# Split attention scores: three single-pass products of high and low parts in place of one four-pass float32 product, and a new table for the order of the work

## The chip, the cores and the metric

The kernel runs on one core of one Trainium2 chip. The metric is the device time of one launch in microseconds (us). Before the change the median of three runs is 1307.7 us (1306.86 to 1309.71).

## The reference

Eight batches of eight heads of attention over 576 tokens with head size 64, in which only scores within `tau` of a row's largest score take part, and then a gated layer over the 4608 tokens (512 wide, 1536 inside):

```python
scores = scale * np.matmul(q, k.transpose(0, 1, 3, 2))
thresh = np.max(scores, axis=-1, keepdims=True) - tau
scores = np.where(scores >= thresh, scores, -1000000000.0)
scores = scores - np.max(scores, axis=-1, keepdims=True)
attn = np.exp(scores)
attn = attn / (np.sum(attn, axis=-1, keepdims=True) + 1e-09)
out = np.matmul(attn, v)            # then (batch, token, head*64) as x
gate = 1.0 / (1.0 + np.exp(-(x @ w_gate)))
val = x @ w_val
return (gate * val @ w_out)
```

## The kernel before

**Attention.** There are 32 visits, one for each batch and each pair of heads; visit n is batch n // 4, pair n % 4. A visit has nine score tiles of 128 query rows by 576 keys: four for each head, and one in which the 64 leftover rows of both heads stand together. q and k come from memory with the head's 64 numbers on 64 partitions, and the two halves of the 576 keys lie on partitions 0 to 63 and 64 to 127. So a tile is computed by two matmuls of 64x128 by 64x288, one on each half of TensorE's rows (line 641); the leftover tile takes four. They are float32 matmuls, and the trace has two records for each. A visit thus has ten pairs of such matmuls and 40 records. After a tile, VectorE takes the row's largest score (L648) and the threshold (L657), ScalarE the exponential (L662), VectorE masks and sums (L665), TensorE turns the result (L756, evicted by ScalarE in L704) and multiplies it by v (L795). GpSimd multiplies a finished visit by the reciprocals of the row sums (L695), which make a round trip through memory to be spread over partitions (tiles `rd` and `rb`).

`plain_scores` loads k (two tiles `kp`, one for each head) and q (`qp`, both heads) and multiplies q by 1/8 in place: on ScalarE or, for visits 1, 2, 4 and all from 6 on, on GpSimd (L621, two instructions a visit).

**The gated layer.** Its products are taken as three fp32r products: an operand is written as a high part (a copy to the type fp32r) and a low part (the operand minus the high part, a subtraction on GpSimd or VectorE), and high x high, high x low and low x high are summed. Part of it stands between the visits: block 0 (L937 in, L866 out), blocks 1 and 2 (L892 in; L866 out, tiles `gpp` and `wpair`), the first two kinds in row halves as well. Blocks 3 to 8 come behind attention in three pairs (L1213 and L1355). The weights come in a packed form and are first converted (`convert`, 36 times, two VectorE instructions each, L528 and L534), and sums of weights and of activations that the pairs need are made on GpSimd (L1071, L1083, L1121, L1126).

**The order.** Every operation is recorded with an engine, a cost and a key. `Plan.run` plays them through with these costs and gives each engine's instructions a fixed order: of the ready operations the one with the smallest key for which there is room in the buffers (`SLOTS`, a number of buffers for each tag). The DMAs all stand in one queue, SP's. Keys of attention are the number of the tile since the start; the gated layer's matmuls have keys from a million up, so they fill what attention leaves. `held_by` ties a visit's scores to the progress of the gated layer. `LAG` is how long a result is taken to need to another engine, `SWITCH` what a change between TensorE's row, column and full forms is taken to cost. Each visit has a seed (`ORDERS`), and all keys below 398 of that visit are moved by random numbers up to 3 drawn from it (`vary`).

The names that the rows below use: `kp`, `qp` are k and q of a visit, `p` the probabilities, `pt` their transposes, `xf` a visit's output, `x` and `wi` the operands of blocks 0 to 2, `s` and `s_o` the sums of weights, `st` the row maxima and thresholds.

Of the kernel before, what the change touches and what calls it, by code (L numbers as in the profile page):

```python
# [4 lines left out]

# [39 lines left out]
class Plan:  # L45

    IN_TURN = ("x", "xf", "kd", "qd", "vs", "p", "pt", "pl", "ptc")

    def __init__(self, pools, slots):
        self.pools, self.slots = pools, slots
# [4 lines left out]
    def buf(self, tag, shape, dtype, name, cls=None):  # L57
        return Buf(self, tag, shape, dtype, name, cls)
# [40 lines left out]
        self.ops.append(o)  # L99
        return o  # L100

    def vary(self, seed):

        draw = random.Random(seed)
        self.nudge = (lambda: draw.uniform(-NUDGE, NUDGE)) if seed else lambda: 0.0

    def room(self, o):
        need = {}
# [150 lines left out]
EARLY = 16  # L259
AHEAD = 5  # L260

PAD = 64

def Q_BY(pair):
    return "POOL" if pair in (1, 2, 4) or pair > 5 else "ACT"
# [25 lines left out]
def LO_DVE(j, out):  # L291
# [2 lines left out]

DVE_LO_IN, DVE_LO_OUT = (), ()

LAG = {"PE": 0.3, "DVE": 0.06, "ACT": 0.08, "POOL": 0.12, "SP": 0.08}

WARM = 16

# [3 lines left out]
    "s": [{0, 1}, {2, 3}, {4, 5}, {6, 7}],  # L304
    "b": [{6}, {7}, {4}, {5}, {2}, {3}, {0}, {1}],
}
STAY, SWITCH, TURN = 4, 0.15, 0.0615
S_CAP, T_CAP, L_CAP, MOE_CAP = (4, 3), 1, 1, 2

MM_HALVES = 0.234  # L310
WHOLE, FULL_STEP = (0,), 6

ORDERED, NUDGE = 398, 3.0
ORDERS = (
    9752, 0, 748, 1675, 6489, 1465, 5011, 3559, 9165, 5460, 4071, 9213, 3320, 7371, 6555, 4493,
    0, 1253, 2636, 4108, 9865, 7590, 738, 2276, 1215, 1549, 3530, 2072, 647, 565, 5179, 0,
)

def LATE(b, hp):
# [21 lines left out]
def act(n):  # L341
    return 0.19 + 0.0008 * n
# [6 lines left out]
def pool(n):  # L349
    return 0.2 + 0.0022 * n  # L350
# [7 lines left out]
def kernel(  # L358
# [208 lines left out]
    class Visit:  # L567
# [28 lines left out]
        def plain_scores(self, key, n):  # L596

            pair = 4 * self.b + self.hp
            self.k1 = [buf("qd", [P, HALF + SL], F32, f"kp{n}_{h}") for h in range(2)]
            qn = self.q1 = buf("kd", [P, 2, SK], F32, f"qp{n}")  # L600

            pieces = [(0, 2 * P), (2 * P, SK)] if n == "0_0" else [(0, SK)]
            for hs in [(0,), (1,)] if n == "0_0" else [(0, 1)]:
                for x in hs:
                    op("SP", 0.7, key - 4 + x, lambda x=x: nc.sync.dma_start(out=self.k1[x].ap, in_=k0[pair, :, x]),
                       writes=[self.k1[x]])
                h = slice(hs[0], hs[-1] + 1)
                for j, (c0, c1) in enumerate(pieces if 0 in hs else [(0, SK)]):
                    parts = [(qn, (x, y)) for x in hs for y in ((j,) if len(pieces) > 1 and 0 in hs else (0, 1))]
                    op("SP", 1.05 * len(hs) * (c1 - c0) / SK, key - 4, lambda h=h, c0=c0, c1=c1: nc.sync.dma_start(  # L610
                        out=qn.ap[:, h, c0:c1], in_=q0[pair, :, h, c0:c1]
                    ), writes=parts)
            for h in range(2):
                for j, (c0, c1) in enumerate(pieces if h == 0 else [(0, SK)]):
                    dst = [(qn, (h, y)) for y in ((j,) if len(pieces) > 1 and h == 0 else (0, 1))]
                    if Q_BY(pair) == "ACT":
                        op("ACT", act(c1 - c0), key + h, lambda h=h, c0=c0, c1=c1: nc.scalar.activation(
                            qn.ap[:, h, c0:c1], qn.ap[:, h, c0:c1], AF.Copy, scale=scale_t[:, 0:1]
                        ), writes=dst)
                        continue  # L620
                    op("POOL", 0.89, key + h, lambda h=h, c0=c0, c1=c1: nc.gpsimd.tensor_scalar(  # L621
                        out=qn.ap[:, h, c0:c1], in0=qn.ap[:, h, c0:c1], scalar1=scale_t[:, 0:1], scalar2=zero_t[:, 0:1],
                        op0=ALU.mult, op1=ALU.add,
                    ), writes=dst)

    def tile_steps(vis, g, i, key):

        h, qt = g.h, g.tiles[i]
        n = f"{g.name}{i}"


# [13 lines left out]

        op("PE", P_COST * len(heads), key, scores, reads=reads, writes=[s], also=[g.p], after=held_by(vis), mode="row")
# [747 lines left out]
    def two_blocks(k):  # L1394

        key = 400 + k
        tags = ["x"] * 6 + ["vs"] * 2 + ["kd"] * 3 + ["p"] * 3
        if k in xs_d:
            tags = ["kd"] * 3 + ["p"] * 3 + ["vs"] * 2 + ["x"] * 6
# [8 lines left out]
                b, d = xt[prod][c].b, xs_d[k][prod, c]  # L1408
                op("SP", 1.7, key, lambda b=b, d=d: nc.sync.dma_start(out=f32(b.ap), in_=d.t), reads=[d], writes=[b])
        else:  # L1410
            base = {}
            tags = iter(["qd"] * 6 + ["xf"] * 2)
            for hp in (0, 2, 1, 3):
                for z in range(2):
                    base[hp, z] = pair_x(k, hp, z, next(tags), key)
# [189 lines left out]
```

## Time and profile before

| | before |
|---|---|
| median of 3 runs | 1307.7 us |
| profiled execution | 1305.66 us |
| its span, first to last instruction | 1303.6 us |
| TensorE (PE) busy | 1265.9 us, 97% |
| VectorE (DVE) busy | 892.8 us, 68% |
| ScalarE (ACT) busy | 685.4 us, 53% |
| GpSimd (POOL) busy | 512.8 us, 39% |
| granted TensorE clock, mean | 0.993 |

The profiled execution took 2.06 us more than its span, and is 2.04 us below the median. "PEld" is TensorE's weight loads, which have a record each and run beside the matmuls. Matmuls overlap one another in TensorE's pipeline, so the mean length of a matmul's record is not the time that it takes from the engine; that is read from the distance between the starts of groups in the chain of waits.

### The profile page before, as it was taken

How to read it: one execution, taken by the hardware profiler on the slowest of the kernel's cores; microseconds unless marked ns; L12 is line 12 of the kernel's file. 1: busy time of each engine (PE TensorE's matmuls, PEld its weight loads, DVE VectorE, ACT ScalarE, POOL GpSimd, SP SyncE). 2: the span in 40 equal slices, each digit the busy share in tenths (PEclk: the TensorE clock that was granted, in tenths of full speed). 3: DMA queues.
4: the chain of work that ended last, by engine and by line, in shares of the span. 5: the costliest groups of instructions: out<-in, count | busy, mean ns of one | idle time of the engine just before them, and what ended most of it. 6: DMA issues, size and time to landing. Idle time of an engine off the chain costs nothing.

```text
span 1303.6 us, 27638 instructions
## 1 busy us (share of the span) xinstructions
PE 1265.9 (97%) x10596; PEld 997.8 (77%) x10596; DVE 892.8 (68%) x1811; ACT 685.4 (53%) x1144; POOL 512.8 (39%) x501
## 2 busy tenths in 40 slices
PE   7879999999999999999999999999999999999998
PEld 5557777777777777777777767888888888888887
DVE  7878887576776766767777774548954579555494
ACT  6877776666665656665776651224522235312242
POOL 4567777665444366584868400111001100010100
PEclk8989999999999999999999999999999999999999
DMA  7669986677655767887446668666676666765663
GB/s 284 218 216 305 337 283 218 225 263 237 234 191 180 236 222 255 288 296 227 156 146 202 222 222 295 195 201 209 221 270 195 198 206 203 232 197 188 203 208 113
DMA packets 134571, 293.17 MB, mean 225 GB/s; under 512 B 27304, under 2 KB 62376, under 8 KB 134440
## 3 DMA queue, kind: packets, MB, share of 16 engines
q1 hardware_dynamic: 134296, 291.41, 67.5%
q8 instruction: 84, 1.38, 0.4%
q14 instruction: 47, 0.39, 0.1%
q10 hardware_dynamic: 144, 0.00, 0.0%
HBM read 229.34 MB, written 62.01 MB: 224 GB/s over the span
## 4 chain that ended last, share of the span: by engine, by line
PE 86%; DMA 3%; DVE 3%; POOL 2%; ACT 2%; issue 2%; SPq 1%; DVEq 0%; POOLq 0%; ACTq 0%
PE banks L1213 26%; PE banks L1355 13%; PE banks L795 11%; PE banks L892 11%; PE banks L641 10%; PE banks L756 5%; PE banks L866 5%; PE banks L937 4%; DMA rb<-rd 1%; DVE p L665 1%; ACT pt L704 1%; DMA xa<-xf 1%; DVE st L648 1%; DMA sod<-s_o 0%; DMA qp<-in_q_dram 0%
## 5 line engine op out<-in xcount | busy, mean ns | idle before, releaser
L648 DVE TENSOR_REDUCE st<-banks 128x1 f32<-128x576 f32 x256 | 190.3, 753 | 142.3 <-PE banks L641 136.5
L665 DVE SCALAR_TENSOR_TENSOR p<-banks,st,p 128x576 f32<-128x576 f32 x256 | 205.0, 813 | 25.2 <-ACT p L662 18.3
L641 PE MATMUL banks<-kp,qp 64*128 64x288 f32 x1280 | 204.2, 424 | 12.9 <-DVE p L665 6.5
L662 ACT ACTIVATE p<-banks,st 128x576 f32<-128x576 f32 x256 | 186.7, 742 | 49.8 <-DVE st L648 48.4
L1126 POOL TENSOR_TENSOR gA<-gA 128x512 f32<-128x512 f32 x18 | 24.2, 1347 | 412.9 <-DVE gA L1192 412.9
L892 PE MATMUL banks<-x,wi 64*128 64x512 f32 x1152 | 178.6, 423 | 3.5 <-DVE g L998 2.5
L1355 PE MATMUL banks<-gs_p,wo_p 128*128 128x512 f32 x756 | 172.3, 389 | 0.0
L1355 PEld LDWEIGHTS banks<-gs_p,wo_p 128*128 128x128 f32 x756 | 141.9, 188 | 29.4
L641 PEld LDWEIGHTS banks<-kp,qp 64*128 64x128 f32 x1280 | 113.5, 189 | 49.7 <-DVE p L665 14.5
L704 ACT COPY pt<-banks 128x1024 f32<-128x1024 f32 x128 | 129.5, 1012 | 35.3 <-PE banks L756 33.3
L892 PEld LDWEIGHTS banks<-x,wi 64*128 64x128 f32 x1152 | 111.3, 186 | 25.9 <-DVE g L998 5.1
L795 PE MATMUL banks<-pt,vs 128*64 128x256 f32 x1024 | 124.7, 386 | 5.6 <-DVE p L665 3.9
L756 PEld LDWEIGHTS banks<-ident,p 64*128 64x128 f32 x2304 | 98.2, 141 | 35.3 <-DVE p L665 5.1
L1150 DVE TENSOR_TENSOR qu<-banks,qp 128x512 f32<-128x512 f32 x72 | 49.8, 692 | 92.9 <-PE banks L1213 74.4
L756 PE MATMUL banks<-ident,p 64*128 64x64 f32 x2304 | 106.1, 227 | 6.1 <-DVE p L665 2.6
L1213 PE MATMUL banks<-xs_p,wa 128*128 128x512 f32 x432 | 110.2, 390 | 0.0
L1213 PE MATMUL banks<-xs_p,wt 128*128 128x512 f32 x432 | 109.2, 389 | 0.0
L795 PEld LDWEIGHTS banks<-pt,vs 128*64 128x64 f32 x1024 | 69.9, 138 | 47.2 <-DVE p L665 5.9
L1213 PE MATMUL banks<-xs_p,ws 128*128 128x512 f32 x432 | 104.1, 390 | 0.0
L1213 PEld LDWEIGHTS banks<-xs_p,wa 128*128 128x128 f32 x432 | 80.8, 188 | 17.8 <-issue 1.2
L1213 PEld LDWEIGHTS banks<-xs_p,ws 128*128 128x128 f32 x432 | 80.9, 188 | 17.5 <-issue 0.7
L1213 PEld LDWEIGHTS banks<-xs_p,wt 128*128 128x128 f32 x432 | 81.1, 188 | 16.9
(125 smaller groups left out, 1991.0 us busy)
## 6 DMA issues: line engine op xcount, KB each, us to landing
wi<-wid SPq DMA_DIRECT2D x48, 512.0 KB
qp<-in_q_dram SPq DMA_DIRECT2D x31, 640.0 KB
wa<-wid SPq DMA_DIRECT2D x36, 512.0 KB
ws<-sid SPq DMA_DIRECT2D x36, 512.0 KB
wt<-sid SPq DMA_DIRECT2D x36, 512.0 KB
wo_p<-sod SPq DMA_DIRECT2D x36, 512.0 KB
wo_p<-wod SPq DMA_DIRECT2D x27, 512.0 KB
vs<-in_v_dram SPq DMA_DIRECT2D x32, 384.0 KB
```

Of the source, the lines that this page charges most:

```text
L641: nc.tensor.matmul(s.ap[:, c, :HALF], vis.q1.ap[rows, x, c0 : c0 + P], vis.k1[x].ap[rows, kc : kc + HALF], start=x == heads[0][0], stop=x ...
L648: op("DVE", 0.76, key, lambda: nc.vector.tensor_reduce(out=st.ap[:, 0:1], in_=sv(), axis=AX.XY, op=ALU.max, negate=True), reads=[s], write ...
L662: op("ACT", 0.74, key, lambda: nc.scalar.activation(p(), sv(), AF.Exp, bias=st.ap[:, 0:1], scale=1.0), reads=[s, (st, 0)], writes=[(g.p, i)])
L665: mask = op("DVE", 0.9, key, lambda: nc.vector.scalar_tensor_tensor(out=p(), in0=sv(), scalar=st.ap[:, 1:2], in1=p(), op0=ALU.is_ge, op1=A ...
L704: op("ACT", act(n), key, lambda: nc.scalar.copy(dst(), src()), reads=at, writes=[part])
L756: nc.tensor.matmul(banks[z]()[:, m * D : (m + 1) * D], p.ap[rows, o : o + P], ident[rows, rows], is_transpose=True, start=m == 0, stop=m = ...
L795: nc.tensor.matmul(av.get()[h * D : (h + 1) * D, a:z], vis.vs.ap[:, j, h], m(h), start=i == 0, stop=i == len(ms) - 1, skip_group_check=True,)
L866: nc.tensor.matmul(acc.ap, w()[h], x()[h], start=start, stop=stop, skip_group_check=True)
L892: nc.tensor.matmul(acc.ap, w()[ROWS[z]], x()[ROWS[z]], start=e == 0 and z == 0, stop=e == n - 1 and z == 1, skip_group_check=True,)
L937: nc.tensor.matmul(m.ap, wv[:, a, c * P : (c + 1) * P], xs[c].ap[:, z, c0:c1], start=e == 0, stop=e == 11,)
L1213: nc.tensor.matmul(acc.ap, wv[:, y, (2 * h + c) * P : (2 * h + c + 1) * P], xt[prod][c].get()[:, z], start=e == 0 and prod in FIRST, stop= ...
L1355: nc.tensor.matmul(acc.ap, w.ap[:, e, c, y], gt[prod][2 * g + c].get()[:, z], start=m == 0 and g == 0 and prod in FIRST, stop=m == 5 and g ...
```

## The change

Visits 0 to 7 keep the float32 scores. For visits 8 to 31 (`NPS` = 8) `split_scores` loads k and q raw (`kr`, `qr`), scales k by 1/8 on GpSimd, copies both to fp32r on ScalarE (`kh`, `qh`) and subtracts on GpSimd (`kl`, `ql`); a score tile is then six fp32r matmuls of 64x128 by 64x288, three on each half of the rows. k of a visit is one buffer of both heads. The buffers change to `kd` 4 (from 3), `qd` 4 of twice the size (from 6), a new `qr` of 2, and fewer of `sm`, `st`, `pl` and `t2`. The seeds give way to a string of letters for each visit, one letter for each recorded key, worth -3 to +3.25; `LAG` of TensorE goes from 0.3 to 0.05 and `SWITCH` from 0.15 to 0.095. In the two last pairs of blocks the loads of the operands (`pair_x`) are recorded ahead of the tiles that are made of them.

```diff
-    def vary(self, seed):
-        draw = random.Random(seed)
-        self.nudge = (lambda: draw.uniform(-NUDGE, NUDGE)) if seed else lambda: 0.0
+    def vary(self, letters):
+        left = iter(letters)
+        self.nudge = lambda: (ord(next(left, "m")) - ord("m")) / 4
...
-    "kd": 3, "qd": 6, "vs": 3,
-    "p": 4, "pc": 1, "sm": 8, "st": 8, "pt": 5, "pl": 3, "ptc": 1, "xf": 2, "rb": 1, "x": 6, "g": 12,
-    "w": 9, "t2": 8,
+    "kd": 4, "qd": 4, "qr": 2, "vs": 3,
+    "p": 4, "pc": 1, "sm": 2, "st": 4, "pt": 5, "pl": 2, "ptc": 1, "xf": 2, "rb": 1, "x": 6, "g": 12,
+    "w": 9, "t2": 6,
...
+NPS, S_COST = 8, 0.4
...
-LAG = {"PE": 0.3, "DVE": 0.06, "ACT": 0.08, "POOL": 0.12, "SP": 0.08}
+LAG = {"PE": 0.05, "DVE": 0.06, "ACT": 0.08, "POOL": 0.12, "SP": 0.08}
...
-STAY, SWITCH, TURN = 4, 0.15, 0.0615
+STAY, SWITCH, TURN = 4, 0.095, 0.0615
...
-    9752, 0, 748, 1675, 6489, 1465, 5011, 3559, 9165, 5460, 4071, 9213, 3320, 7371, 6555, 4493,
+    "aurjgowpymjncypethhjkwwkslfdheenhoeocwdmcuayyefyypouxekbbfmpttkylomujcngsxtho",
...
+        def split_scores(self, pair, key, n):
+            kr = buf("qr", [P, 2, HALF + SL], F32, f"kr{n}")
+            qr = [buf("qr", [P, SK], F32, f"qr{n}_{h}") for h in range(2)]
+            kh, kl = (buf("qd", [P, 2, HALF + SL], F32R, f"k{z}{n}") for z in "hl")
+            qh, ql = (buf("kd", [P, 2, SK], F32R, f"q{z}{n}") for z in "hl")
+            self.ks, self.qs = [kh, kl], [qh, ql]
+            W = 2 * (HALF + SL)
+            op("SP", 1.2, key - 4, lambda: nc.sync.dma_start(out=kr.ap, in_=k0[pair]), writes=[kr])
+            for h in range(2):
+                op("SP", 1.05, key - 4, lambda h=h: nc.sync.dma_start(out=qr[h].ap, in_=q0[pair, :, h]), writes=[qr[h]])
+            op("POOL", 0.95, key - 1, lambda: nc.gpsimd.tensor_scalar(
+                out=kr.ap, in0=kr.ap, scalar1=scale_t[:, 0:1], scalar2=zero_t[:, 0:1], op0=ALU.mult, op1=ALU.add,
+            ), writes=[kr])
+            op("ACT", act(W), key - 1, lambda: nc.scalar.copy(kh.ap, kr.ap), reads=[kr], writes=[kh])
+            op("POOL", pool(W), key - 1, lambda: nc.gpsimd.tensor_tensor(
+                out=kl.ap, in0=kr.ap, in1=f32(kh.ap), op=ALU.subtract
+            ), reads=[kr, kh], writes=[kl])
+            for h in range(2):
+                parts = [(h, 0), (h, 1)]
+                op("ACT", act(SK), key + h, lambda h=h: nc.scalar.copy(qh.ap[:, h], qr[h].ap),
+                   reads=[qr[h]], writes=[(qh, y) for y in parts])
+                op("POOL", pool(SK), key + h, lambda h=h: nc.gpsimd.tensor_tensor(
+                    out=ql.ap[:, h], in0=qr[h].ap, in1=f32(qh.ap[:, h]), op=ALU.subtract
+                ), reads=[qr[h]] + [(qh, y) for y in parts], writes=[(ql, y) for y in parts])
...
+        terms = [(0, 0)] if vis.plain else [(0, 0), (0, 1), (1, 0)]
...
-            for (x, c0), c in itertools.product(heads, range(2)):
+            first, last = (heads[0][0], terms[0]), (heads[-1][0], terms[-1])
+            for (x, c0), (a, z), c in itertools.product(heads, terms, range(2)):
...
-                    s.ap[:, c, :HALF], vis.q1.ap[rows, x, c0 : c0 + P], vis.k1[x].ap[rows, kc : kc + HALF],
-                    start=x == heads[0][0], stop=x == heads[-1][0], skip_group_check=True,
+                    s.ap[:, c, :HALF], form(vis.qs[a].ap[rows, x, c0 : c0 + P]),
+                    form(vis.ks[z].ap[rows, x, kc : kc + HALF]),
+                    start=(x, (a, z)) == first, stop=(x, (a, z)) == last, skip_group_check=True,
```

TensorE's order where the first scores of visit 17 stand (`kp_1`, `qp_1`; `kh_1`, `kl_1`, `qh_1`, `ql_1` after), between matmuls of the gated layer (`x`, `wi`). Before:

```order
L892 MATMUL banks<-x_3_3060,wi_10_0_5286 128x512
L641 MATMUL banks<-kp_1_0_5095,qp_1_5113 128x288 x2
L641 MATMUL banks<-kp_1_1_5122,qp_1_5113 128x288 x2
L892 MATMUL banks<-x_0_1914,wi_9_0_5540 128x512
L892 MATMUL banks<-x_0_1914,wi_10_1_5451 128x512
```

And now:

```order
L959 MATMUL banks<-x_3_3220,wi_10_1_5743 128x512
L707 MATMUL banks<-kh_0_5519,qh_0_5550 128x288 x2
L707 MATMUL banks<-kl_0_5537,qh_0_5550 128x288 x2
L707 MATMUL banks<-kh_0_5519,ql_0_5569 128x288 x2
L707 MATMUL banks<-kh_1_5934,qh_1_5985 128x288 x2
L707 MATMUL banks<-kl_1_5958,qh_1_5985 128x288 x2
L707 MATMUL banks<-kh_1_5934,ql_1_6033 128x288 x2
L959 MATMUL banks<-x_0_1815,wi_9_1_5904 128x512
```

A pair of float32 matmuls has become three pairs of fp32r matmuls that take all their operands from the four split buffers; what stands around them is of the same kind.

GpSimd's order behind the multiplication of a finished visit in the same part of the program (`xf` is a finished visit, `s` the sums of weights, line 621 the scaling of q). Before:

```order
L695 TENSOR_TENSOR xf_1_5082<-xf_1_5082,rb_1_4958 128x576
L621 TENSOR_SCALAR qp_1_5113<-qp_1_5113,scale_t,zero_t 128x640 x2
L1071 TENSOR_TENSOR s_8_0_5277<-wi_8_0_5165 128x512
L1071 TENSOR_TENSOR s_8_0_5370<-wi_10_0_5286 128x512
L1071 TENSOR_TENSOR s_8_0_5277<-s_8_0_5370 128x256
L1071 TENSOR_TENSOR s_8_0_5277<-s_8_0_5277 128x256
L1071 TENSOR_TENSOR s_8_0_5370<-s_8_0_5277,s_8_0_5370 128x256
L1071 TENSOR_TENSOR s_8_0_5370<-s_8_0_5277 128x256
L1083 TENSOR_TENSOR s_8_0_5277<-s_8_0_5277 128x512
L1083 TENSOR_TENSOR s_8_0_5370<-s_8_0_5370 128x512
L695 TENSOR_TENSOR xf_2_5434<-xf_2_5434,rb_2_5319 128x576
```

And now:

```order
L762 TENSOR_TENSOR xf_1_5393<-xf_1_5393,rb_1_5371 128x576
L1138 TENSOR_TENSOR s_5_0_5413<-s_5_0_5220,s_5_0_5413 128x256
L1138 TENSOR_TENSOR s_5_0_5413<-s_5_0_5220 128x256
L678 TENSOR_TENSOR kl_0_5537<-kr_0_5353,kh_0_5519 128x704
L685 TENSOR_TENSOR ql_0_5569<-qr_0_0_5368,qh_0_5550 128x640
L1150 TENSOR_TENSOR s_5_0_5220<-s_5_0_5220 128x512
L1138 TENSOR_TENSOR s_8_0_5641<-wi_8_0_5302 128x512
L1138 TENSOR_TENSOR s_8_0_5673<-wi_10_0_5566 128x512
L685 TENSOR_TENSOR ql_0_5569<-qr_0_1_5573,qh_0_5550 128x640
L674 TENSOR_SCALAR kr_1_5605<-kr_1_5605,scale_t,zero_t 128x704
L1150 TENSOR_TENSOR s_5_0_5413<-s_5_0_5413 128x512
```

Four instructions of a visit's preparation stand where two stood, spread between the sums, and each subtraction has a copy on ScalarE ahead of it and a load on SP's queue behind it.

## Rows read from the trace of the kernel before

**Rows 1.** The page, parts 1 (busy us, share, instructions) and 4 (chain by engine).

```profile
PE 1265.9 (97%) x10596; PEld 997.8 (77%) x10596; DVE 892.8 (68%) x1811; ACT 685.4 (53%) x1144; POOL 512.8 (39%) x501
...
PE 86%; DMA 3%; DVE 3%; POOL 2%; ACT 2%; issue 2%; SPq 1%; DVEq 0%; POOLq 0%; ACTq 0%
```

**Rows 2.** Four stretches: length, busy us of PE, PEld, DVE, ACT, POOL; clock, DMA.

```profile
core 0: us, PE busy (x) PEld busy (x) DVE busy (x) ACT busy (x) POOL busy (x), PEclk, DMA share, GB/s
0.00:100.00 100.00, 78.39 (x856) 55.61 (x857) 78.63 (x172) 73.62 (x115) 56.79 (x90) 0.91 0.70 240
100.00:200.00 100.00, 99.82 (x757) 70.44 (x757) 82.20 (x164) 75.77 (x123) 74.74 (x69) 1.00 0.90 309
200.00:770.00 570.00, 560.45 (x6558) 438.04 (x6554) 398.15 (x969) 371.55 (x628) 331.30 (x306) 1.00 0.67 221
770.00:1304.00 534.00, 527.21 (x2434) 433.71 (x2430) 333.79 (x509) 164.46 (x279) 49.95 (x37) 1.00 0.65 210
```

**Rows 3.** Chain of waits, 400 to 412 us: start, length, engine, tile, line, records.

```profile
401.27 0.98 PE banks L892 x8
...
402.74 0.54 PE banks L641 x4
403.28 1.85 PE banks L892 x16
405.13 0.48 PE banks L641 x4
...
408.99 0.97 PE banks L641 x8
```

**Rows 4.** Groups of instructions, 200 to 770 us, PE and its weight loads.

```profile
L892 PE MATMUL banks<-x,wi 64*128 64x512 f32 x1152 | 178.6, 423 | 3.5 <-DVE g L998 2.5 <-ACT th L995 1.0
...
L641 PE MATMUL banks<-kp,qp 64*128 64x288 f32 x984 | 153.6, 416 | 3.0 <-issue 1.0 <-DVE p L665 0.9 <-ACT pl L704 0.5
...
L892 PEld LDWEIGHTS banks<-x,wi 64*128 64x128 f32 x1152 | 111.3, 186 | 25.9 <-DVE g L998 5.1 <-ACT th L995 3.0 <-ACT ot L1036 0.2
...
L641 PEld LDWEIGHTS banks<-kp,qp 64*128 64x128 f32 x984 | 87.9, 186 | 27.2 <-DVE p L665 5.8 <-ACT pt_l L704 2.3 <-issue 2.3
```

**Rows 5.** The same view, POOL and ACT.

```profile
L704 ACT COPY pt<-banks 128x1024 f32<-128x1024 f32 x97 | 98.1, 1011 | 23.6 <-PE banks L756 22.3 <-DVE st L657 0.6
...
L1121 POOL TENSOR_TENSOR gpp<-g,gpp 128x512 fp32r<-128x512 f32 x36 | 45.4, 1282 | 27.8 <-ACT gpp L1118 27.8
...
L621 POOL TENSOR_SCALAR qp<-qp,scale_t,zero_t 128x640 f32<-128x640 f32 x44 | 38.3, 879 | 50.5 <-DMA qp<-in_q_dram 40.5 <-PE banks L756 8.5 <-PE banks L641 1.5
L695 POOL TENSOR_TENSOR xf<-xf,rb 128x576 f32<-128x576 f32 x25 | 35.5, 1419 | 62.1 <-ACT xf L821 34.2 <-DMA rb<-rd 25.8 <-ACT p L662 1.9
...
L1071 POOL TENSOR_TENSOR s<-s 128x256 f32<-128x256 f32 x36 | 26.5, 735 | 1.7
...
L1118 ACT CAST gpp<-g 128x512 fp32r<-128x512 f32 x42 | 24.4, 623 | 1.4 <-PE banks L866 1.4
...
L704 ACT COPY pt_l<-banks 128x640 f32<-128x640 f32 x25 | 17.3, 694 | 0.7 <-PE banks L756 0.5
```

**Rows 6.** Who waited for whom on POOL: us in total, times, longest.

```profile
POOL xf L695 <- DMA rb<-rd: 47.8, 10, 21.0
POOL qp L621 <- DMA qp<-in_q_dram: 44.4, 15, 10.4
...
POOL xf L695 <- ACT xf L821: 34.2, 10, 16.7
```

**Rows 7.** Groups of instructions over the whole span: conversion on DVE.

```profile
L528 DVE SCALAR_TENSOR_TENSOR banks<-banks,wa 128x512 int32<-128x512 int32 x36 | 24.9, 692 | 2.5 <-POOL wa L521 0.9 <-ACT banks L525 0.8 <-issue 0.5
...
L534 DVE SCALAR_TENSOR_TENSOR wa<-wr,banks 128x512 int32<-128x512 int32 x36 | 24.7, 687 | 1.1
```

**Rows 8.** Two stretches of 10 us in the start; columns as in rows 2.

```profile
10.00:20.00 10.00, 6.31 (x64) 4.23 (x62) 8.28 (x18) 5.64 (x8) 6.33 (x12) 0.76 1.03 415
...
60.00:70.00 10.00, 6.97 (x84) 4.84 (x82) 9.05 (x22) 7.54 (x12) 4.40 (x10) 1.00 0.29 103
```

More of the change, by code (lines that the diff above doesn't have):

```diff
@@ L2 @@
 import itertools
-import random
 from contextlib import ExitStack
@@ L45 @@
 class Plan:
-    IN_TURN = ("x", "xf", "kd", "qd", "vs", "p", "pt", "pl", "ptc")
+    IN_TURN = ("x", "xf", "kd", "qd", "qr", "vs", "p", "pt", "pl", "ptc")
     def __init__(self, pools, slots):
@@ L260 @@
 AHEAD = 5
-PAD = 64
+PAD = 56
+NPS, S_COST = 8, 0.4
 def Q_BY(pair):
@@ L598, in plain_scores @@
             pair = 4 * self.b + self.hp
-            self.k1 = [buf("qd", [P, HALF + SL], F32, f"kp{n}_{h}") for h in range(2)]
-            qn = self.q1 = buf("kd", [P, 2, SK], F32, f"qp{n}")
+            self.plain = pair < NPS
+            if not self.plain:
+                self.split_scores(pair, key, n)
+                return
+            kk = buf("qd", [P, 2, HALF + SL], F32, f"kp{n}")
+            qn = buf("kd", [P, 2, SK], F32, f"qp{n}")
+            self.ks, self.qs = [kk], [qn]
             pieces = [(0, 2 * P), (2 * P, SK)] if n == "0_0" else [(0, SK)]
@@ L604, in plain_scores @@
                 for x in hs:
-                    op("SP", 0.7, key - 4 + x, lambda x=x: nc.sync.dma_start(out=self.k1[x].ap, in_=k0[pair, :, x]),
-                       writes=[self.k1[x]])
+                    op("SP", 0.7, key - 4 + x, lambda x=x: nc.sync.dma_start(out=kk.ap[:, x], in_=k0[pair, :, x]),
+                       writes=[(kk, x)])
                 h = slice(hs[0], hs[-1] + 1)
@@ L635, in tile_steps @@
         heads = [(0, SM), (1, SM)] if h is None else [(h, qt * P)]
-        reads = [y for x, c0 in heads for y in ((vis.q1, (x, int(c0 >= 2 * P))), vis.k1[x])]
+        reads = [y for x, c0 in heads for q in vis.qs for y in [(q, (x, int(c0 >= 2 * P)))] + [(k, x) for k in vis.ks]]
+        terms = [(0, 0)] if vis.plain else [(0, 0), (0, 1), (1, 0)]
+        form = lambda ap: ap
         def scores():
-            for (x, c0), c in itertools.product(heads, range(2)):
+            first, last = (heads[0][0], terms[0]), (heads[-1][0], terms[-1])
+            for (x, c0), (a, z), c in itertools.product(heads, terms, range(2)):
                 rows = slice(c * D, (c + 1) * D)
                 nc.tensor.matmul(
-                    s.ap[:, c, :HALF], vis.q1.ap[rows, x, c0 : c0 + P], vis.k1[x].ap[rows, kc : kc + HALF],
-                    start=x == heads[0][0], stop=x == heads[-1][0], skip_group_check=True,
+                    s.ap[:, c, :HALF], form(vis.qs[a].ap[rows, x, c0 : c0 + P]),
+                    form(vis.ks[z].ap[rows, x, kc : kc + HALF]),
+                    start=(x, (a, z)) == first, stop=(x, (a, z)) == last, skip_group_check=True,
                 )
-        op("PE", P_COST * len(heads), key, scores, reads=reads, writes=[s], also=[g.p], after=held_by(vis), mode="row")
+        op("PE", (P_COST if vis.plain else S_COST) * len(heads), key, scores, reads=list(dict.fromkeys(reads)), writes=[s], also=[g.p], after=held_by(vis), mode="row")
         st = buf("st", [P, 2], F32, f"st{n}")
@@ L1396, in two_blocks @@
         key = 400 + k
+        if k not in xs_d:
+            base = {}
+            tags = iter(["qd"] * 4 + ["xf"] * 2 + ["qr"] * 2)
+            for hp in (0, 2, 1, 3):
+                for z in range(2):
+                    base[hp, z] = pair_x(k, hp, z, next(tags), key)
         tags = ["x"] * 6 + ["vs"] * 2 + ["kd"] * 3 + ["p"] * 3
@@ L1410, in two_blocks @@
         else:
[L1411 to L1415, printed above, removed]
             for c in range(2):
```

34 lines of the change are left out of this document (32 added, 2 removed).

## The prediction

> **What bounds the kernel now.** I read the page's busy shares and its chain of waits first. TensorE is busy 97% of the span and the chain runs through it for 86%; no other engine is over 68% [rows 1]. So the time is TensorE's work plus its idle time, and the next view is where it idles. By stretches: 21.6 of the first 100 us, 0.2 of the next 100, 9.6 of the 570 in which most of attention stands between matmuls of the gated layer, and some 6 in the last stretch, where only the gated layer is left [rows 2]. In the middle stretch a microsecond taken from TensorE's work is a microsecond of time, as long as the others still deliver. They have room: VectorE is busy 70% of it, ScalarE 65%, GpSimd 58% [rows 2].
>
> **What a score costs.** TensorE's price is the distance between starts in the chain. Four float32 records, one pair of matmuls on the two row halves, take 0.48 to 0.54 us, and eight take 0.97 [rows 3]; I take 0.485 a pair, which is four passes of 288 columns at 2.4 GHz (0.480) and hardly more. In the same chain sixteen fp32r records of 512 columns, eight pairs, take 1.85 us, 0.231 a pair, and eight take 0.98, 0.245 a pair [rows 3]: one pass of 512 columns at 2.4 GHz (0.213) and 0.018 to 0.032 more.
>
> **The new score.** Three fp32r pairs of 288 columns have no row. By the share of the columns a pair is 0.231 x 288/512 = 0.130, three are 0.390. With the 0.018 as a fixed cost a pair is 0.120 + 0.018 = 0.138, three are 0.414. The ends are 3 x 0.120 = 0.360, nothing but columns, and 3 x 0.231 = 0.693, if a pair of 288 columns takes no less than one of 512. I take 0.400, between the two scalings of the nearest row. The gain is 0.085 a pair; 24 visits with ten pairs make 240, so **-20.4 us** (the scalings give -17 to -23, the ends -30 and +50). All of it lies on the path, since the split visits stand in the stretch where TensorE is 98% busy.
>
> The bound that matters is the weight load. Each product brings one, 0.186 us in its record [rows 4], and the new pairs would follow one another every 0.13 to 0.14 us. The rows show loads hidden: in the stretch the 512-column pairs come every 0.231 us, though a load of 0.186 and a pass of 0.213 one behind the other would need 0.399. What they don't show is a hidden load that is longer than the pass beside it. The Trainium skill has a rule against this change (TensorE: Matmul & The Clock Gate, "Part 3: Packing small matmuls", "The mechanism"): a weight load overlaps matmuls in flight only where its row group differs. By its load figure of 128 columns at 1.2 GHz, 107 ns, a pair would be about 0.227 and three 0.68, an estimate of +47 us in all. The distance of 0.231 in this trace speaks against the rule, since it too would be 0.320 by it.
>
> **What is added beside it.** GpSimd: two scalings of 0.879 a visit go [rows 5]. There come one scaling of 704 columns (0.879 x 704/640 = 0.97), one subtraction of 704 and two of 640. Two-input subtractions take 0.735 at 256 columns, 1.282 at 512 and 1.419 at 576 [rows 5], 2.14 ns a column, so 1.69 and twice 1.56. That is 5.8 a visit in place of 1.8: +4.0, 96 us over 24 visits. GpSimd goes from 331 to about 427 of some 550 us, 78%. ScalarE: copies of 640 columns take 0.694 and of 1024 1.011, and a cast to fp32r of 512 takes 0.623 [rows 5]; so 0.75 + 2 x 0.69 = 2.1 a visit, 51 us, to 423 of 550, 77%. Both hide under TensorE, and the loads of k and q move the same bytes. The cover is the lead: a visit's splits are ordered one visit, some 22 us, ahead of its scores. If it goes, GpSimd's 5.8 us or a part of them stand before a visit's first scores.
>
> It is not free, because an engine that is fuller answers later. GpSimd keeps its order, and it already waits for transfers with everything behind it: ten times for the reciprocals, 47.8 us, at most 21.0, and 15 times for q, 44.4 us [rows 6]. What stands behind such a wait now is 5.8 us of splits where it was 1.8 of scaling, and who waits for them is TensorE's next visit. The raw buffers are two for three loads a visit, so the second half of q is only loaded once a subtraction has let a buffer go, and behind that load on SP's queue stand the weight streams of the gated layer. A transfer that waits there makes the next weights late, for which the prefetch of five units is the cover. Bounds: TensorE's idle time of 9.6 us in the stretch stays, or it doubles. I take **+3**.
>
> **The start.** The first 100 us have the float32 scores still, and change by the new table alone. TensorE waits there for VectorE and ScalarE: in 60 to 70 us VectorE is busy 9.05 of 10 and TensorE 6.97 [rows 8]. By the order, two, four and five weight conversions have passed VectorE when the second, third and fourth visit end; now one, two and four. A conversion takes 0.69 + 0.69 us there [rows 7], so I take **-1.4** at the end of the fourth visit, with bounds of 8 us to either side (a third of the 21.6 idle), since a random table moves everything. At 10 to 20 us the transfers are full (DMA share 1.03, granted clock 0.76 of the 2.4 GHz level) [rows 8], and both orders load the same there.
>
> **The end.** Two temporaries fewer (`t2` 6) could hold the last chains; by the order, TensorE's instructions of the last two pairs of blocks are the same, row for row, and the stretch has 6 us of idle time with VectorE at 63% [rows 2]. I take 0, with at most +3. Of the smaller `sm` and `st` I expect nothing: a tile keeps its `st` no longer than its scores, of which only four can stand at once.
>
> **Sum.** -20.4 + 3 - 1.4 = -18.8 on the profiled execution's 1305.66 us: 1286.9. That execution lies 2.0 below the median, so **1289 us**.
>
> **Rivals.** *Everything lands well:* the three pairs near 0.37 (-28), no more idle time, -5 in the start: 1275. For it: float32's own four passes show hardly any overhead at 288 columns [rows 3]. Against it: the fp32r pairs do show some.
>
> *Given back:* the product pairs at 0.14 and the idle time doubled: -15 + 9.6, with 0 in the start, so about 1302, from 1296 to 1307. For it: GpSimd's waits for transfers [rows 6], which no engine's speed shortens. Against it: TensorE found other work through those waits in the middle stretch.
>
> *GpSimd's line, the slower side:* a visit's subtractions stand behind the multiplication of a finished visit, and that waits for its reciprocals. If the ten waits of 4.8 us each come through to TensorE in full, because the one-visit lead is used up, that is +48 on -18.8: 1337. It decides from the point where the splits of most visits end behind the place of their first scores, which needs about 0.8 us a visit (18.8/24) to be slower than before. For it: the longest waits, 21.0 and 16.7 us [rows 6], are about as long as the lead. Against it: 22% of GpSimd would still be free, and filling matmuls need none of these splits.
>
> *Weight loads come to the surface:* load and pass of a half one behind the other, 0.186 + 0.120 = 0.306 a pair, three 0.918; +104 on TensorE, so about 1413. This is what the rule of the Trainium skill named above (TensorE: Matmul & The Clock Gate) would make of these rows. The same side holds the case that the change doesn't do what it says, the fp32r products streaming at float32's four passes, 3 x 0.485: +233. Against both stand the 0.231 us of a 512-column pair.
>
> **How the numbers follow.** The forecast has 0.58, with a range of its own from 1281 to 1296 (the two scalings, and 0 to 8 us more idle time); everything well 0.14; given back 0.16; GpSimd's line 0.08; the loads 0.04. About 0.2% is what a measurement of this kernel can tell from no change, 1305 to 1310 us. "Given back" is faster with 0.11 of its 0.16 and within 0.2% with the rest. So faster 0.83, same 0.06, slower 0.11 (two cases of the slower side, less rounding). The range from 1271 to 1309 leaves out the slower side and the far end of the good case.
>
> **What would show it.** Right: the first scores of a visit come as groups of six records every 0.39 to 0.41 us in the chain, TensorE's busy time falls by about 20 us, GpSimd's rises by 96 and ScalarE's by 51, and TensorE's idle time between 200 us and the end of attention stays under 15. Wrong: six records that take over 0.45 us (the price of a pair), TensorE's loads or scores waiting for the new subtractions on GpSimd (the lead), matmuls of the gated layer waiting for `wi` (SP's queue behind the raw loads), or a first 100 us in which the idle time has moved by more than 8.

## The result, and the profile after

| | before | changed |
|---|---|---|
| median of the runs (lowest to highest) | 1307.28 us (1304.38 to 1309.71) | **1295.10 us** (1293.94 to 1295.74) |
| ratio | | 0.9907, 95% interval 0.9885 to 0.9928 |
| span of the profiled execution | 1303.6 us | 1292.1 us |

The change gains 12.2 us; 18.8 were forecast. The page of the changed kernel, parts 1 and 4, answers to [rows 1]:

```profile
PE 1253.0 (97%) x11076; PEld 1003.6 (78%) x11076; DVE 893.9 (69%) x1811; ACT 729.2 (56%) x1216; POOL 607.0 (47%) x549
...
PE 88%; ACT 3%; DVE 3%; DMA 2%; issue 2%; POOL 1%; SPq 0%; DVEq 0%; POOLq 0%; ACTq 0%
```

GpSimd is 94.2 us busier (96 forecast), ScalarE 43.8 (51 forecast), TensorE 12.9 less busy, where 20 less were expected. Where the rest went shows when the span is cut at the end of the last matmul of attention, at 781.42 us before and 760.85 after. By windows, first the kernel before, then the changed one (columns as in [rows 2]: stretch, its length, busy time of PE, PEld, DVE, ACT, POOL, then clock and DMA):

```profile
100.00:781.42 681.42, 670.11 (x7435) 515.42 (x7433) 489.08 (x1152) 451.23 (x756) 406.04 (x374) 1.00 0.70 235
781.42:1303.60 522.18, 517.37 (x2309) 426.76 (x2308) 325.06 (x488) 160.56 (x273) 49.95 (x37) 1.00 0.64 208
```

```profile
0.00:100.00 100.00, 79.43 (x862) 54.92 (x864) 78.59 (x172) 74.32 (x114) 57.14 (x91) 0.95 0.73 249
100.00:760.85 660.85, 649.36 (x7912) 520.44 (x7910) 487.78 (x1152) 494.39 (x829) 499.95 (x421) 1.00 0.73 241
760.85:1292.10 531.25, 524.25 (x2308) 428.25 (x2308) 327.56 (x488) 160.45 (x273) 49.92 (x37) 1.00 0.64 206
```

Attention is 20.57 us shorter, with as much idle time as before (11.49 us against 11.31). The end is **9.07 us longer**: 2.2 are idle time, and 6.9 are busy time of TensorE *with the same instructions*. That second part is the case's riddle.

A score in the timeline of TensorE (start, busy time, engine, line, operation, tiles, records):

```profile
403.92 0.62 PE L959 MATMUL banks<-x,wi 64*128 64x512 f32 x4
404.38 0.29 PE L707 MATMUL banks<-kh,qh 64*128 64x288 f32 x2
404.51 0.30 PE L707 MATMUL banks<-kl,qh 64*128 64x288 f32 x2
404.64 0.30 PE L707 MATMUL banks<-kh,ql 64*128 64x288 f32 x2
404.77 2.02 PE L959 MATMUL banks<-x,wi 64*128 64x512 f32 x16
```

Read the starts, not the busy times: 404.38, .51, .64, .77. A pair of products comes every 0.13 us, three in 0.39; 0.40 was taken. The busy times of 0.30 overlap and can't be added.

This is a group that nothing disturbs, and not every group is one. In the chain of waits of the changed kernel (start, length, engine, tile, line, records) a score of six records takes 0.40 or 0.45 us, two take 1.06 and three 1.25:

```profile
402.83 1.25 PE banks L707 x18
...
404.54 0.40 PE banks L707 x6
...
413.17 0.45 PE banks L707 x6
...
422.14 1.06 PE banks L707 x12
```

A piece of the chain runs from the end of one group to the end of the next. Added up like that over all records of the trace, from 100 us to the end of attention and without idle time, the 1440 records of the 240 split scores take 106.9 us, **0.445 a score**. The kernel before has 1088 float32 records there with 144.5 us; the changed kernel keeps 128 of them with 18.7, so the 960 that went took 125.8 us, **0.524 a pair**. The gain in the scores' own records is 18.9 us, 0.079 a pair, of the 20.8 us by which TensorE's busy time falls in attention. The ends of matmuls are modelled, so how the time is divided between neighbouring rows is an estimate; the 20.8 are not.

The weight loads of these products, and GpSimd's new operations, in the groups of 200 to 770 us:

```profile
L707 PEld LDWEIGHTS banks<-kl,qh 64*128 64x128 f32 x480 | 47.7, 186 | 2.4
...
L685 POOL TENSOR_TENSOR ql<-qr,qh 128x640 fp32r<-128x640 f32 x46 | 72.0, 1565 | 32.0 <-ACT qh L683 28.1 <-ACT seen L971 3.8
...
L678 POOL TENSOR_TENSOR kl<-kr,kh 128x704 fp32r<-128x704 f32 x23 | 39.2, 1706 | 15.5 <-ACT kh L677 9.1 <-PE banks L707 6.4
...
L674 POOL TENSOR_SCALAR kr<-kr,scale_t,zero_t 128x704 f32<-128x704 f32 x22 | 20.5, 932 | 3.7 <-DMA kr<-in_k_dram 3.6
```

A load's record is 0.186 us, longer than the 0.13 from one pair to the next, and it stays hidden. A visit costs GpSimd 0.93 + 1.71 + 2 x 1.57 = 5.77 us (5.8 forecast).

Now the end. The same stretch of it in the timeline, before (the first fence) and after:

```profile
1062.77 2.88 PE L1213 MATMUL banks<-xs_p,ws 128*128 128x512 f32 x12
1065.49 1.52 PE L1213 MATMUL banks<-xs_p,wa 128*128 128x512 f32 x6
1066.85 1.52 PE L1213 MATMUL banks<-xs_p,wt 128*128 128x512 f32 x6
1068.21 2.88 PE L1355 MATMUL banks<-gs_p,wo_p 128*128 128x512 f32 x12
```

```profile
1048.76 2.88 PE L1280 MATMUL banks<-xs_p,ws 128*128 128x512 f32 x12
1051.48 1.55 PE L1280 MATMUL banks<-xs_p,wa 128*128 128x512 f32 x6
1052.87 1.56 PE L1280 MATMUL banks<-xs_p,wt 128*128 128x512 f32 x6
1054.27 2.90 PE L1422 MATMUL banks<-gs_p,wo_p 128*128 128x512 f32 x12
```

Before, six products take 1.36 us from start to start here. After, the twelve with `ws` take 2.72 as before, but the six with `wa` take 1.39 and the six with `wt` 1.40. The granted clock is 1.00 in both, and TensorE waits for nothing there. The other part is one wait, in the list of waits (engine, tile and line, what for, total, times, longest):

```profile
PE banks L1280 <- DMA ws<-sid: 3.1, 1, 3.1
```

The wait costs more than its idle time: behind it the granted clock falls, which the 1.00 of the whole end hides. Two windows of the changed kernel (length, TensorE's busy time and records, clock, DMA), and the timeline of the same stretch:

```profile
774.00:778.00 4.00, 0.93 (x5) 1.00 1.02 405
778.00:782.00 4.00, 4.00 (x12) 0.57 1.07 398
```

```profile
777.59 2.34 PE L1280 MATMUL banks<-xs_p,ws 128*128 128x512 f32 x6 [3.07 <-DMA ws<-sid]
779.72 3.84 PE L1280 MATMUL banks<-xs_p,wt 128*128 128x512 f32 x12
783.40 2.88 PE L1280 MATMUL banks<-xs_p,wd 128*128 128x512 f32 x12
```

TensorE is busy for 0.93 of 4 us, and then the clock averages 0.57, so most of the next 4 us are at the 1.2 GHz level. The six products take 2.13 us in place of 1.36, the next twelve 3.68 in place of 2.72 to 2.79. Added up, the products at the low clock cost 1.6 us more than at 226.7 ns each. So of the 6.9 us of busy time about 5.3 are left to explain.

### The profile page after: what moved, and what is told of

Its sections match the earlier page's. It is cut to its first block, busy times and chain, and to the rows that moved or that the text cites. A ratio compares the mean times of both kernels' runs of the same rounds, so it can differ in the third digit from the quotient of the medians.

```text
span 1292.1 us, 28801 instructions
## 1 busy us (share of the span) xinstructions
PE 1253.0 (97%) x11076; PEld 1003.6 (78%) x11076; DVE 893.9 (69%) x1811; ACT 729.2 (56%) x1216; POOL 607.0 (47%) x549
## 4 chain that ended last, share of the span: by engine, by line
PE 88%; ACT 3%; DVE 3%; DMA 2%; issue 2%; POOL 1%; SPq 0%; DVEq 0%; POOLq 0%; ACTq 0%
PE banks L1280 27%; PE banks L1422 13%; PE banks L862 11%; PE banks L707 10%; PE banks L959 10%; PE banks L823 6%; PE banks L933 6%; PE banks L1004 5%; ACT pt L771 1%; DVE p L732 1%; DVE st L715 1%; DMA ws<-sid 1%; ACT p L729 1%; POOL gpp L1188 0%; DMA sod<-s_o 0%
## 5 line engine op out<-in xcount | busy, mean ns | idle before, releaser
L1422 PE MATMUL banks<-gs_p,wo_p 128*128 128x512 f32 x756 | 173.8, 391 | 0.0
L959 PE MATMUL banks<-x,wi 64*128 64x512 f32 x1152 | 165.7, 401 | 0.5 <-ACT seen L971 0.4
L1422 PEld LDWEIGHTS banks<-gs_p,wo_p 128*128 128x128 f32 x756 | 142.0, 188 | 30.9
L823 PEld LDWEIGHTS banks<-ident,p 64*128 64x128 f32 x2304 | 95.1, 140 | 36.4 <-DVE p L732 6.6
L959 PEld LDWEIGHTS banks<-x,wi 64*128 64x128 f32 x1152 | 106.4, 186 | 15.3 <-ACT th L1062 0.9
L1280 PE MATMUL banks<-xs_p,wa 128*128 128x512 f32 x432 | 111.9, 394 | 0.0
L1280 PE MATMUL banks<-xs_p,wt 128*128 128x512 f32 x432 | 111.6, 395 | 0.0
L1280 PE MATMUL banks<-xs_p,ws 128*128 128x512 f32 x432 | 105.5, 393 | 3.1 <-DMA ws<-sid 3.1
L1185 ACT CAST gs_p<-gA 128x512 fp32r<-128x512 f32 x72 | 43.7, 620 | 96.2 <-DVE gA L1259 51.0
L1280 PEld LDWEIGHTS banks<-xs_p,ws 128*128 128x128 f32 x432 | 81.2, 189 | 21.2 <-DMA ws<-sid 3.5
L1280 PEld LDWEIGHTS banks<-xs_p,wt 128*128 128x128 f32 x432 | 82.0, 190 | 18.7
L1280 PEld LDWEIGHTS banks<-xs_p,wa 128*128 128x128 f32 x432 | 80.8, 188 | 18.5 <-issue 0.3
L685 POOL TENSOR_TENSOR ql<-qr,qh 128x640 fp32r<-128x640 f32 x48 | 75.2, 1566 | 32.0 <-ACT qh L683 28.1
```

Source lines behind the costliest of these rows:

```text
L685: op("POOL", pool(SK), key + h, lambda h=h: nc.gpsimd.tensor_tensor(out=ql.ap[:, h], in0=qr[h].ap, in1=f32(qh.ap[:, h]), op=ALU.subtract), ...
L823: nc.tensor.matmul(banks[z]()[:, m * D : (m + 1) * D], p.ap[rows, o : o + P], ident[rows, rows], is_transpose=True, start=m == 0, stop=m = ...
L959: nc.tensor.matmul(acc.ap, w()[ROWS[z]], x()[ROWS[z]], start=e == 0 and z == 0, stop=e == n - 1 and z == 1, skip_group_check=True,)
L1280: nc.tensor.matmul(acc.ap, wv[:, y, (2 * h + c) * P : (2 * h + c + 1) * P], xt[prod][c].get()[:, z], start=e == 0 and prod in FIRST, stop= ...
L1422: nc.tensor.matmul(acc.ap, w.ap[:, e, c, y], gt[prod][2 * g + c].get()[:, z], start=m == 0 and g == 0 and prod in FIRST, stop=m == 5 and g ...
```

## The experiments

The kernel before ran beside every group of them, at medians of 1307.28 to 1307.73 us, so times of different groups are compared as they are.

**The place of the tiles.** In the built programs (start of a tile in bytes of its partition) the kernel before has all large tiles 64 bytes past a multiple of 256: `kd` 16192, `w` 62528, `x` 200256. In the changed kernel `kd` (15136) and `vs` (35616) are 32 past one, `p` (48032), `w` (66464), `pt` (103328) and `x` (204704) 160 past one. Four `st` tiles of 32 bytes in place of eight lie between. My first guess was coarser: that every start off a multiple of 64 bytes is slow. The changed kernel with its unused constant tile at 64 floats again (e1) has no room, 220.19 kb a partition where 220.16 are left, and gives no time; so the guess was tried on the kernel before:

```diff
-PAD = 64
+PAD = 56
```

> The kernel before with the unused constant tile at 56 floats instead of 64: same order on every engine, all large tiles 32 bytes off a multiple of 64 bytes, as in the changed kernel. Theory of the addresses: groups of twelve products of 512 columns rise from 2.72 to 2.74 to 2.80 us, the end grows by about 5 us from 522.2, and the median rises from 1307 to 1312 to 1318. Rival (what runs beside the products): 1306 to 1308, no change.

1306.98 us, ratio 0.9994 (0.9981 to 1.0007): the theory of a common start off 64 bytes falls. The end is as it was, 517.35 us busy of 522.14:

```profile
781.36:1303.50 522.14, 517.35 (x2309) 426.68 (x2308) 324.92 (x488) 160.54 (x273) 49.87 (x37) 1.00 0.64 208
```

So a common place of all tiles is indifferent; what is left is the place of one tile against another. I then noticed that the slow products stream `vs` and `kd` tiles (by the order `wa` multiplies a `vs` tile there, `wt` a `kd` tile, `ws` two pairs of `x` tiles):

```diff
-PAD = 56
+PAD = 24
 ...
+        if b.tag == "st" and not self.gap:
+            self.gap = pool.tile([128, 32], F32, tag="gap", name="gap", bufs=1)
```

> The changed kernel with 128 bytes per partition moved: the unused constant tile shrinks from 56 to 24 floats and an unused tile of 32 floats lies between the st tiles and the p tiles, so that only qd, kd, qr and vs tiles and the small ones before them lie 128 bytes lower. The order on every engine is the same. In the changed kernel the kd and vs tiles start 32 bytes past a multiple of 256 and all the other large tiles 160 bytes past one, and the matmuls of the end that stream kd or vs tiles against w tiles are the ones that begin the slow stretches; in the kernel before all large tiles start 64 bytes past a multiple of 256. Theory (a matmul streams slower when its moving tile and its weight tile start at different places of 256 bytes): 226.7 ns for every product of 512 columns, TensorE's busy time behind attention back from 524.25 to 517 to 518, the median 1286 to 1290. Rival (the changed kernel's instruction stream or its four kd tiles themselves are slow, not the place): 524 us busy there and 1294 to 1296.

**1289.19 us, ratio 0.9866 (0.9846 to 0.9885)**: faster than both kernels. By windows, attention and the end:

```profile
100.00:761.66 661.66, 650.27 (x7918) 519.06 (x7917) 489.18 (x1154) 495.34 (x830) 501.49 (x423) 1.00 0.74 241
761.66:1285.60 523.94, 517.11 (x2309) 426.71 (x2308) 326.27 (x488) 160.37 (x273) 49.95 (x37) 1.00 0.65 209
```

TensorE's busy time in the end is back from 524.25 to 517.11, and attention is within 1 us of what it was. (The `qr` tiles lie behind the unused tile and stay where they were, other than the expectation says.) About 1.6 us of the return are the clock: the wait for `ws` is still there, but the clock does not fall behind it. The reverse, on the kernel before:

```diff
+        if b.tag == "st" and not self.gap:
+            self.gap = pool.tile([128, 32], F32, tag="gap", name="gap", bufs=1)
```

> The kernel before with one unused tile of 32 floats between its st and its p tiles and nothing else: qd, kd and vs tiles stay 64 bytes past a multiple of 256, p, w, pt, g and x tiles now start 192 bytes past one. Theory of the places: TensorE's busy time behind attention rises from 517.4 to 522 to 525 and the median from 1307 to 1311 to 1316. Rival: no change, 1306 to 1308.

1313.16 us, ratio 1.0040 (1.0025 to 1.0055), 5.7 slower by one unused tile. TensorE's busy time in the end rises by 5.5 us, without a fall of the clock there:

```profile
783.66:1311.30 527.64, 522.86 (x2308) 426.90 (x2308) 326.14 (x488) 160.66 (x273) 49.96 (x37) 1.00 0.64 206
```

With the unused tile at 16 floats, and at 64:

> As e6, but the unused tile has 16 floats: p, w, pt, g and x tiles start 128 bytes past a multiple of 256, qd, kd and vs tiles 64. If any difference of places costs: TensorE's busy time behind attention 520 to 525 again. If only places 128 bytes apart (two of four 64-byte steps) cost: 517.4, as in the kernel before.

> As e6, but the unused tile has 64 floats, so that the tiles behind it move by 256 bytes and all large tiles keep the same place of 256 (64 bytes past a multiple). If the place within 256 bytes decides: 517.4 busy behind attention, as in the kernel before. If any gap between the tiles costs, or the place within a longer stretch: 520 to 525.

One run each: 1314.93 and 1305.72 us. In the end (the first fence is 64 bytes, the second 256):

```profile
784.36:1312.80 528.44, 523.70 (x2309) 426.28 (x2308) 326.18 (x488) 160.62 (x273) 49.82 (x37) 1.00 0.64 206
```

```profile
781.47:1303.60 522.13, 517.38 (x2308) 426.62 (x2308) 325.03 (x488) 160.55 (x273) 49.94 (x37) 1.00 0.64 208
```

TensorE's busy time in the end is 523.70 and 517.38 us, against 517.37 in the kernel before. So 64 and 128 bytes cost, 256 cost nothing: it is the place within 256 bytes, not a gap. 192 bytes were not tried.

**What a product is worth.**

```diff
-        terms = [(0, 0)] if vis.plain else [(0, 0), (0, 1), (1, 0)]
+        terms = [(0, 0)] if vis.plain else [(0, 0), (0, 1)]
```

> The changed kernel without the product of the high part of k and the low part of q in visits 8 to 31, the low part still being made: 480 of 1440 fp32r products of scores left out, everything else in the same order. Theory (TensorE bounds attention and a product of two passes of 288 columns costs 0.13 to 0.14 us there): 240 x 0.13 = 31 us less, 1262 to 1268. Rival (feeding bounds it: GpSimd's and ScalarE's lines or DMA set the pace of visits 8 to 31, so that freed TensorE time turns into waits): 1280 to 1295, with TensorE's idle time in 200:770 up by about as much as its work falls.

1277.28 us, ratio 0.9777 (0.9750 to 0.9804): 17.8 below the changed kernel, between the two theories. By windows:

```profile
100.00:741.95 641.95, 627.52 (x7435) 487.07 (x7434) 487.51 (x1153) 493.68 (x830) 499.68 (x422) 1.00 0.76 249
741.95:1276.00 534.05, 525.20 (x2308) 428.75 (x2308) 327.60 (x488) 160.46 (x273) 49.89 (x37) 0.99 0.63 204
```

TensorE's work in attention falls by 21.8 us (0.091 a pair, not 0.13), its idle time rises from 11.5 to 14.4, and 2.8 more are lost in the end. The scores' own records do take 29.2 us less (77.7 for 106.9, added up as above), 0.122 a pair, near the price of 0.13; but the rows between them take some 7 us more, and no run shows why. That part my 31 us had left out. TensorE's work was still the larger part of what set the pace.

**What the letter table is worth.** First the changed kernel without letters, then the kernel before without seeds:

```diff
-        self.nudge = lambda: (ord(next(left, "m")) - ord("m")) / 4
+        self.nudge = lambda: 0.0
```

> The changed kernel with the letter table ignored (each nudge is 0), so that the planner's own order stands; the split scores stay. If the price of the scores is the gain and the table only trims waits: 1297 to 1315, TensorE's idle time up by 2 to 20 us, score groups still at 0.40 to 0.42 us a pair. Rival (the table carries the gain and the split by itself gains nothing): at or above the 1307 of before, with idle time that eats all of the 20 us.

```diff
-        self.nudge = (lambda: draw.uniform(-NUDGE, NUDGE)) if seed else lambda: 0.0
+        self.nudge = lambda: 0.0
```

> The kernel before with its random nudges off (every nudge is 0), so that the planner's own order stands, as e4 did for the changed kernel (1342). If the split of the scores is worth its 20 us in whatever order: 1357 to 1367, 15 to 25 us above e4. If order and split belong together (without letters the split's extra work on GpSimd and ScalarE eats the gain): 1330 to 1348, about e4's time.

1342.44 us (ratio 1.0270, 1.0241 to 1.0298) and 1331.13 us (1.0193, 1.0169 to 1.0217). e4 is on its rival's side, far beyond what I had put for the price of the scores alone, and e7 lies where order and split belong together. The seeds were worth 24 us to the kernel before, the letters 47 to the changed one, and *in the planner's own order the split kernel is 11 us slower*. That is not the split alone: the two kernels also differ in `LAG`, `SWITCH`, the buffer counts, the order of the `pair_x` loads and the places of the tiles, and no run takes these apart. By windows of attention, e4 and then e7:

```profile
100.00:800.40 700.40, 667.23 (x7879) 521.61 (x7879) 487.12 (x1157) 499.06 (x831) 497.56 (x418) 0.99 0.69 226
```

```profile
100.00:793.74 693.74, 670.84 (x7400) 512.34 (x7400) 483.96 (x1151) 447.57 (x747) 404.98 (x374) 1.00 0.68 225
```

Idle time is 33.2 us without letters and 22.9 without seeds, where 11.5 and 11.3 stand with them. TensorE's work is only 3.6 us less with the split, not 20.8; some 7 us of that are the clock, 0.99 over 700 us. At 760 to 780 us of e4 few of the layer's matmuls are left to fill with (54 records of `L933` in the 20 us before; 8, and 24 of `L1280`, in the 40 us after), TensorE is busy 14.96 of 20 us after 18.20 of 20, and the granted clock averages 0.83, so a part of the stretch is at the 1.2 GHz level:

```profile
740.00:760.00 20.00, 18.20 (x246) 14.86 (x246) 16.39 (x42) 16.24 (x26) 6.19 (x4) 1.00 0.65 198
760.00:780.00 20.00, 14.96 (x160) 11.69 (x158) 13.66 (x35) 10.35 (x15) 1.41 (x1) 0.83 0.38 120
```

**GpSimd's slack.**

```diff
-            op("POOL", pool(W), key - 1, lambda: nc.gpsimd.tensor_tensor(
+            op("POOL", pool(W), key - 1, lambda: [nc.gpsimd.tensor_tensor(
                 out=kl.ap, in0=kr.ap, in1=f32(kh.ap), op=ALU.subtract
-            ), reads=[kr, kh], writes=[kl])
+            ) for _ in range(2)][1], reads=[kr, kh], writes=[kl])
```

> The changed kernel in which GpSimd makes each low part of k twice in the same step (24 x 1.42 us = 34 us more on GpSimd, in the same order on every engine). Theory (GpSimd has slack until about 600 us and is full only in 600 to 700): +2 to +8 us, 1297 to 1303, the loss in 600 to 700. Rival of the prediction (GpSimd's line sets the pace of the visits): +20 to +34 us, 1315 to 1329.

1304.15 us, ratio to the kernel before 0.9985 (0.9968 to 1.0002), 9.05 above the changed kernel, one more than my theory's upper end and far from the rival:

```profile
100.00:768.89 668.89, 653.59 (x7899) 522.91 (x7896) 487.93 (x1151) 495.29 (x829) 540.35 (x445) 0.99 0.73 238
768.89:1302.10 533.21, 525.20 (x2309) 428.74 (x2308) 327.63 (x488) 160.53 (x273) 49.94 (x37) 0.99 0.64 205
```

GpSimd is 40 us busier in attention (1.7 us for each of 24 more subtractions), and TensorE's idle time there rises from 11.5 to 15.3. The other 4.2 us that attention grows by are busy time, with the clock at 0.99. About three quarters of the added work stays hidden: the cover is real, but not free. The loss is not where my theory put it: in 600 to 700 us the idle time falls from 4.66 to 4.01 us, in 400 to 600 it rises from 2.56 to 4.95.

**Taking work from GpSimd**, on top of e5:

```diff
-PAIR_BY, PAIR_KEY = (("POOL",) * 4, ("POOL",) * 6 + ("DVE",)), 399
+PAIR_BY, PAIR_KEY = (("POOL",) * 4, ("POOL",) * 3 + ("DVE",) + ("POOL",) * 2 + ("DVE",)), 399
```

> e5 with six more of the 42 low parts of the output pair's sums (L1188 of the changed kernel) on VectorE instead of GpSimd (PAIR_BY's second list: GpSimd 3, VectorE 1, GpSimd 2, VectorE 1), to take 6 x 1.4 = 8 us from GpSimd in 600 to 700, where it is 94% busy and TensorE idles 5 us. The planner orders the work after about 650 us anew. Theory (GpSimd full is what costs there): 1285 to 1288. Rival (the late order is worse without its letters, or VectorE becomes late): 1290 to 1300.

1341.35 us, ratio 1.0247 (1.0231 to 1.0264): beyond both ranges, on the rival's side. The code has the cause: `token_sums` makes every VectorE instruction of these sums wait for the masks of the last visit (`behind = {"POOL": (), "DVE": masked}`). In the instructions on the tile `gpp` from 600 to 800 us (count, ns least, median and most, first and last start):

```profile
L1191 POOL TENSOR_TENSOR gpp<-g,gpp x27: 1266/1284/1304, 605.4 to 793.9; 128x512 fp32r<-128x512 f32 x27
L1191 DVE TENSOR_TENSOR gpp<-g,gpp x6: 681/1752/1759, 766.7 to 772.9; 128x512 fp32r<-128x512 f32 x6
```

VectorE's six come only at 766.7 us, and with them the output pair's matmuls, which should have filled attention; in 700 to 770 TensorE is busy 51.47 of 70 us, at a granted clock of 0.70. The experiment says nothing about GpSimd's price.

## Why the prediction was right or wrong

- **The score's gain: right. Its two prices: both too low.** TensorE's work up to the end of attention falls by (78.39 + 670.11) - (79.43 + 649.36) = 19.7 us (20.4 forecast). Three pairs take 0.39 to 0.40 us where nothing disturbs them (0.400 taken), but 0.445 on the mean of all groups; the float32 pair took 0.524, where 0.485 was taken, the shorter end of [rows 3]. Both prices were those of undisturbed groups. The two errors of 0.04 cancel in the difference (0.079 a pair, 0.085 taken), and that they do is luck. Of the 84 groups of six records that stand alone, 30 are over the 0.45 us that the prediction named as the sign of a wrong price.
- **The weight loads: right.** Pairs come every 0.13 us, with loads of 0.186 us on the same two row groups in turn. The rule of the Trainium skill (TensorE: Matmul & The Clock Gate, "Part 3: Packing small matmuls", "The mechanism"), that a load overlaps matmuls in flight only in another row group, disagrees with this trace. The same section also lets a load run ahead into a background weight buffer, which the prediction left out and which would fit the trace.
- **GpSimd, ScalarE and feeding: right within its bounds.** GpSimd's added work is as forecast, ScalarE's 7 us less. Idle time in attention rose by 0.2 us, where +3 was taken. Part of that is slack (e8 hides three quarters of 40 us more) and part is the table's doing: the letters hold idle time at 11.5 that is 33.2 without them. I had costed the table as -1.4 us in the start and at nothing elsewhere, and the split as a gain of its own; in the planner's own order e7 and e4 show no such gain, and what the split alone is worth stays open.
- **The start: the size is right, the cause is not shown.** TensorE is 1.04 us busier in the first 100 us (1.4 forecast). No run moves the weight conversions alone.
- **The end: wrong, and it is the whole miss.** "I take 0, with at most +3", because TensorE's instructions are the same row for row there. They are, and they took 6.9 us more. About 5.3 of it comes from the edits of the pools, which moved `kd` and `vs` tiles by 128 bytes against the others: e5 takes this back and lands on 1289.2, and e6 makes 5.5 us of it on the kernel before. About 1.6 is the low clock behind the wait for `ws`. The other 2.2 us are idle time, and the new wait of 3.1 for `ws` is more than that; its load was issued at 769.68 us and landed 7.86 later. e5 still has it (2.9 us), and an earlier load was not tried. Smaller idle time than the +3 in attention made up for a part of the 9.1, and so 1295.1 us lies just inside the forecast's range of 1281 to 1296, which had no term for either cause: luck again. The sum: -19.71 - 1.04 + 0.18 + 9.07 = -11.5 us of span (1303.6 to 1292.1).

## What to carry to other kernels

Equal instructions are not equal times: a change of buffer counts moves every tile that is allocated behind them, and where streamed and stationary tiles no longer start at the same place within 256 bytes, the same matmuls can be slower. Compare the start-to-start time of one unchanged group at the same granted clock first; a difference there is no matter of order or waits. And a change that comes with a new order should be tried with the orders of both sides taken out: here that cost 24 and 47 us, more than the change gained.

## What the runs showed of the hardware that I had not expected

- **The place of tiles within 256 bytes.** Products of 512 columns take 226.7 ns each (1.36 us for six) where all large tiles start at the same place within 256 bytes, and 231 to 233 (1.39 to 1.40 for six) in the slow groups where `kd` and `vs` tiles start 128 bytes off the `w` tiles. A common place of 64 (before), 32 (e2) or 160 (e5) makes no difference; 64 (e9) and 128 bytes (e6) apart do, 256 (e10) do not. The built program names both tiles of every product, and that bears out that it is the streamed tile against the weight tile: in the changed kernel's end, leaving out the stretch at the low clock, the 677 products whose two tiles start at different places are 232.6 ns from the next start on the mean, the 1554 others 228.0, and all 2242 of the kernel before 227.0. For the products that stream `kd` and `vs` tiles, e5 moved the streamed tiles and left the `w` tiles, and e6 did it the other way round. A few products behind a slow group are slow as well (the first of `L1422` above); why, no run shows.
- **By starts, part of a float32 score's time stands in the next line's rows.** In the timeline of the kernel before, where the piece of eight records of [rows 3] at 408.99 us stands (the piece begins at the end of the four records before it, 408.14 + 0.84):

```profile
407.29 1.24 PE L641 MATMUL banks<-kp,qp 64*128 64x288 f32 x8
408.14 0.84 PE L892 MATMUL banks<-x,wi 64*128 64x512 f32 x4
408.81 1.14 PE L641 MATMUL banks<-kp,qp 64*128 64x288 f32 x8
```

  Four records of `L892` take 0.67 us behind float32 scores, from 408.14 to 408.81, where four of `L959` take 0.46 in the changed kernel (403.92 to 404.38). So by starts a good part of the gain appears in the layer's rows, not in the scores': their mean fell from 423 ns [rows 4] to 401, as the changed kernel's group below shows. Counted from end to end these rows take the same in both, 144.1 and 143.5 us up to the end of attention, and the gain is in the scores.

```profile
L959 PE MATMUL banks<-x,wi 64*128 64x512 f32 x1152 | 165.7, 401 | 0.5 <-ACT seen L971 0.4
```
